# Toeplitz bands by predicated copies, four half batches fetched in SyncE's order, and passes on zeros ahead of the first convolution

## The chip, the core and the metric

The kernel runs on one core of a Trainium2 chip. The metric is the time of one execution on the device, in microseconds (us). The kernel before took 1273.2 us (median of 3 runs, 1272.89 to 1273.23). The engines are named as in the profile: PE is TensorE, DVE is VectorE, ACT is ScalarE, POOL is GpSimd and SP is SyncE, which only issues transfers.

## What is computed

Every token is a weighted sum of itself and the six tokens ahead of it, with softmax weights of its own for each of eight heads of 24 columns. The 28672 results then go through a mixture of eight experts: logits, a greedy assignment by falling logit with room for 3584 tokens in each expert, and two matrices per expert.

```python
def _attn_ref(x, weight):                      # x (8, 3584, 192), weight (8, 7)
    w = softmax(weight, axis=-1)               # per head
    x_pad = concatenate([zeros(B, 6, D), x], axis=1)
    x_unf = x_pad[:, idx, :].reshape(B, S, K, H, group)     # K = 7 taps, H = 8, group = 24
    return einsum('hk,bskhg->bshg', w, x_unf).reshape(B, S, D)

def _moe_ref(x, w_gate, w1, w2):               # x (28672, 192), w1 (8, 192, 1024), w2 (8, 1024, 192)
    logits = x @ w_gate
    for idx in argsort(-logits.flatten()):
        tok, e = idx // E, idx % E
        if assigned[tok] < 0 and counts[e] < cap:
            assigned[tok] = e
            counts[e] += 1
    for e in range(E):
        mask = assigned == e
        out[mask] = maximum(x[mask] @ w1[e], 0) @ w2[e]
```

## The kernel before

**Half batches.** The sequence work is cut into 16 half batches of 1792 tokens (NHB). In SBUF one is a tile X of 118 partitions by 16 windows by 192 columns: partitions 6 to 117 hold 112 successive tokens of each window, and partitions 0 to 5 hold the six tokens ahead of them (the halo). Four X tiles take turns. One half batch is fetched by three transfers: the halo (69 to 74 KB) and the first eight windows (688 KB) on SyncE's queue, and the other eight windows on ScalarE's (on SyncE's for half batch 0). Every row of 192 columns is a packet of 768 bytes.

**The Toeplitz matrices.** For each head, `toeplitz` builds a 118 by 128 matrix TH[h] that holds the head's seven weights on seven diagonals. The softmax of the weights (tile wb, with wm for maximum and sum) runs on VectorE and ScalarE. MK holds seven masks of one diagonal each. VectorE builds six heads' matrices, in pairs, by one multiplication and six multiply-adds each; ScalarE and GpSimd together build those of heads 1 and 5.

**The convolution.** `conv(i, mid)` runs over the eight heads. Per head TensorE multiplies TH[h] with X's 384 columns of that head into a PSUM bank cv, in two passes since the operands are fp32; `mid(h)` puts in other work; then ScalarE copies cv into the tile a (an evacuation). There are four cv banks and three tiles a. After the eighth head ScalarE issues the store of a to the DRAM tensor attn (1.38 MB, packets of 3 KB). VectorE transposes the a of one half batch while the next one is convolved, TensorE computes its logits (pl) a half batch later, and the logits are transposed (pt) into the table LT. Steps of the expert assignment (thresholds, counts) and, later, of the first expert tiles are put in by `hook`.

**Order.** The main loop calls `k.load(i + 3)` at the start of half batch i, so ScalarE issues its part of X of half batch i + 3 after the store of i - 1 and ahead of the first evacuation of i. Each engine works in the order in which its instructions are written. A transfer issued by SyncE or ScalarE signals one of eight semaphores, which are handed out in turn over both queues; the issue of a transfer waits until the one before it on the same semaphore has landed. An issuing engine does nothing else while it waits.

**The gate.** `gate_ops` loads the gate matrix wgr four times, into four groups of 32 partitions, and GpSimd copies each into its place in GF (in the trace c_mu).

After the loop come the experts' matrices (ph, px and y in the trace), which take most of the time; the change touches nothing of them.

## Time and profile before

| | |
|---|---|
| median of 3 runs | 1273.2 us |
| the profiled execution | 1268.0 us, of which the span is 1266.2 us |
| TensorE busy | 1222.0 us, 97% of the span |
| VectorE / ScalarE / GpSimd busy | 999.6 / 551.2 / 510.1 us |
| start of half batches 0, 1, 2, 3, 4 | 11.61, 20.34, 28.17, 37.79, 47.35 us |

The times of the trace count from the start of the span of that one execution. "Busy" of an engine counts its instructions' own durations, without the issuing of transfers and the waiting for semaphores. A wait is put down to what signalled last. Names such as L55 are lines; since one helper records every operation of the compute engines, most of them have line 55, and the tiles' names tell them apart. L188, L191 and L193 are the three transfers of X, L168 the gate's and L204 the store of a.

### The profile page before, as it was taken

The numbers are of one execution on the slowest core, as the hardware profiler recorded it, in microseconds if no ns is written. First come the engines' busy times: TensorE is split into PE (matmuls) and PEld (weight loads), VectorE is DVE, ScalarE is ACT, GpSimd is POOL, SyncE is SP. The second block draws the span as 40 slices with busy tenths as digits, with TensorE's granted clock in tenths as the row PEclk, the third lists the DMA queues.
The fourth block names the chain that finished last, engine by engine and source line by source line (L and its number), as shares of the span: only waits on it lengthen the run. The fifth ranks groups of instructions, "written<-read, shape, count | busy, mean of one in ns | idle before, by whom it ended". The sixth has DMA issues, their size and how long they took to land.

```text
span 1266.2 us, 21792 instructions
## 1 busy us (share of the span) xinstructions
PE 1222.0 (97%) x7839; PEld 1049.9 (83%) x7839; DVE 999.6 (79%) x2245; ACT 551.2 (44%) x1220; POOL 510.1 (40%) x504
## 2 busy tenths in 40 slices
PE   5889979999999999999999999999999999999997
PEld 2445558899889888887889999999999999999997
DVE  7398669999999989988857777777777777777772
ACT  4544645565544543643433333333333333333332
POOL 3000435364444443533244444444444444444422
PEclk9999989999999999999999999999999999999999
DMA  9999897999533343423653513242314132231100
GB/s 236 347 334 297 271 328 257 294 316 319 194 103 112 122 152 94 152 93 125 161 126 105 205 41 100 94 155 62 129 48 147 46 102 97 85 105 47 45 26 28
DMA packets 100579, 193.02 MB, mean 152 GB/s; under 512 B 19232, under 2 KB 64752, under 8 KB 96240
## 3 DMA queue, kind: packets, MB, share of 16 engines
q1 hardware_dynamic: 57856, 115.15, 28.1%
q0 software_dynamic: 21504, 44.07, 11.7%
q10 hardware_dynamic: 21104, 32.34, 7.8%
q8 instruction: 63, 1.03, 0.3%
q14 instruction: 52, 0.43, 0.1%
HBM read 116.02 MB, written 75.50 MB: 151 GB/s over the span
## 4 chain that ended last, share of the span: by engine, by line
PE 83%; DVE 7%; DMA 5%; issue 1%; POOL 1%; ACT 1%; SPq 1%; POOLq 0%; ACTq 0%; DVEq 0%
PE ph L55 38%; PE y L55 37%; PE cv L55 3%; PE bg L55 3%; DMA X<-in_x_dram 1%; PE px L55 1%; DVE X L55 1%; DMA raw<-in_moe_w_dram 1%; DVE hl L55 1%; DVE oa L55 1%; DVE aT L55 1%; DMA wgr<-in_moe_w_gate_dram 1%; PE pl L55 1%; DMA X<-otab 1%; POOL xg L1262 0%
## 5 line engine op out<-in xcount | busy, mean ns | idle before, releaser
L55 PE MATMUL y<-w,hh 128*128 128x384 f32 x1792 | 539.3, 356 | 0.0
L55 ACT ACTIVATE hh<-ph 128x512 fp32r<-128x512 f32 x448 | 268.1, 598 | 494.2 <-PE ph L55 493.9
L55 PE MATMUL y<-w,hl 128*128 128x192 f32 x1792 | 448.9, 251 | 0.0
L55 DVE SCALAR_TENSOR_TENSOR hl<-ph,hh 128x512 fp32r<-128x512 f32 x448 | 308.1, 688 | 140.6 <-ACT hh L55 136.6
L55 PE MATMUL ph<-xa,w 128*128 128x512 f32 x1344 | 395.7, 402 | 3.9 <-DVE hl L55 3.9
L55 PEld LDWEIGHTS y<-w,hl 128*128 128x128 f32 x1792 | 341.0, 190 | 15.1
L55 PEld LDWEIGHTS y<-w,hh 128*128 128x128 f32 x1792 | 336.4, 188 | 19.1 <-issue 2.3
L1337 POOL DMA_INDIRECT out_dram<-yo,ib x128 | 127.9, 999 | 288.4 <-DVE yo L55 278.6
L55 PEld LDWEIGHTS ph<-xa,w 128*128 128x128 f32 x1344 | 218.7, 189 | 24.6 <-DVE hl L55 5.2
L1337 POOL DMA_INDIRECT out_dram<-yo,ia x96 | 112.2, 1168 | 262.3 <-DVE yo L55 230.0
L55 DVE STREAM_TRANSPOSE xs<-xg 32x256 f32<-32x256 f32 x496 | 182.9, 369 | 8.5
L55 PE MATMUL ph<-xd,w 128*128 128x512 f32 x448 | 177.3, 396 | 1.5 <-DVE xd L55 1.5
L55 PE MATMUL ph<-xd,dl 128*128 128x512 f32 x448 | 174.5, 390 | 0.0
L1262 POOL DMA_INDIRECT xg<-attn,jb x128 | 137.8, 1076 | 40.9 <-issue 40.9
L1262 POOL DMA_INDIRECT xg<-attn,ja x96 | 110.2, 1147 | 32.1 <-issue 26.7
L55 ACT ACTIVATE yt<-y 128x192 f32<-128x192 f32 x224 | 73.6, 328 | 102.6 <-PE y L55 99.5
L55 PE MATMUL cv<-X,TH 118*128 118x384 f32 x256 | 99.6, 515 | 18.9 <-DVE TH L55 12.5
L55 DVE TENSOR_TENSOR yo<-y,yt 128x192 f32<-128x192 f32 x224 | 79.4, 354 | 40.8 <-ACT yt L55 38.1
L55 PEld LDWEIGHTS ph<-xd,w 128*128 128x128 f32 x448 | 84.2, 188 | 21.2 <-DVE xd L55 2.0
L55 PEld LDWEIGHTS ph<-xd,dl 128*128 128x128 f32 x448 | 84.3, 188 | 19.7
L55 PEld LDWEIGHTS cv<-X,TH 118*128 118x128 f32 x256 | 44.6, 194 | 51.8 <-issue 13.0
L55 ACT ACTIVATE a<-cv 128x384 f32<-128x384 f32 x128 | 59.7, 492 | 53.3 <-PE cv L55 32.0
(237 smaller groups left out, 900.4 us busy)
## 6 DMA issues: line engine op xcount, KB each, us to landing
w<-kw SPq DMA_DIRECT2D x16, 1536.0 KB
w<-kv SPq DMA_DIRECT2D x16, 1536.0 KB
attn<-a ACTq DMA_DIRECT2D x16, 1344.0 KB
kw<-w SPq DMA_DIRECT2D x48, 256.0 KB
kv<-w SPq DMA_DIRECT2D x32, 384.0 KB
X<-in_x_dram SPq DMA_DIRECT2D x17, 672.0 KB
X<-in_x_dram ACTq DMA_DIRECT2D x15, 672.0 KB
raw<-in_moe_w_dram SPq DMA_DIRECT2D x32, 192.0 KB
```

Of the source, the lines that this page charges most:

```text
L55: return f(*a, **k)
L1262: self.nc.gpsimd.indirect_dma_start(out=t[:, b], out_offset=None, in_=self.attn[0:rows], in_offset=bass.IndirectOffsetOnAxis(ap=idx[b], ax ...
L1337: st = self.nc.gpsimd.indirect_dma_start(out=self.out, out_offset=bass.IndirectOffsetOnAxis(ap=idx, axis=0), in_=o, in_offset=None, bounds ...
```

## The change

- VectorE sets a tile zb to zero, and TensorE runs 28 passes of 512 bf16 columns on it into the bank pt, ahead of everything else (`warm`).
- The seven diagonals are built only in a band: C has 38 columns per head and partition, and the seven weights are put into it by seven predicated copies, each for all eight heads (304 elements per partition), with MK as an integer mask. Four copies, two on VectorE and two on ScalarE, put C's four groups of 32 partitions in their places in TH, which GpSimd has zeroed whole. The multiply-adds on VectorE and the steps on ScalarE and GpSimd go.
- SyncE issues half batches 0 to 3 whole (halo and all 16 windows in two transfers), with one load of the gate matrix between 1 and 2. The four copies into GF read that one tile and run on VectorE.
- From i = 1 to 12, `load(i + 3)` still issues the halo and the first eight windows at the start of half batch i; ScalarE's part is issued in `mid(3)`, between the third and the fourth evacuation.

SyncE's first issues, before (X_180, X_188, X_278 and X_312 are half batches 0, 1, 2 and 3; a wait names a semaphore):

```order
L188 DMA X_180<-in_x_dram 6x15x192
L193 DMA X_180<-in_x_dram 112x8x192 x2
L191 DMA X_188<-in_x_dram 6x16x192
L193 DMA X_188<-in_x_dram 112x8x192
L168 DMA wgr_141<-in_moe_w_gate_dram 32x6x8 [waits DMAHW0_49]
L168 DMA wgr_141<-in_moe_w_gate_dram 32x6x8 [waits DMAHW1_49]
L168 DMA wgr_141<-in_moe_w_gate_dram 32x6x8 [waits DMAHW2_49]
L168 DMA wgr_141<-in_moe_w_gate_dram 32x6x8 [waits DMAHW3_49]
L188 DMA X_278<-in_x_dram 6x15x192 [waits DMAHW5_49]
L193 DMA X_278<-in_x_dram 112x8x192 [waits DMAHW6_49]
L191 DMA X_312<-in_x_dram 6x16x192 [waits DMAHW0_49]
L193 DMA X_312<-in_x_dram 112x8x192 [waits DMAHW2_49]
```

and with the change (half batches 0, 1, 2 and 3 are X_211, X_215, X_219 and X_223):

```order
L202 DMA X_211<-in_x_dram 6x15x192
L208 DMA X_211<-in_x_dram 112x16x192
L205 DMA X_215<-in_x_dram 6x16x192
L208 DMA X_215<-in_x_dram 112x16x192
L176 DMA wgr_143<-in_moe_w_gate_dram 32x6x8
L202 DMA X_219<-in_x_dram 6x15x192
L208 DMA X_219<-in_x_dram 112x16x192 [waits DMAHW0_49]
L205 DMA X_223<-in_x_dram 6x16x192 [waits DMAHW2_49]
L208 DMA X_223<-in_x_dram 112x16x192 [waits DMAHW4_49]
```

The gate's four loads, each with a wait, no longer stand ahead of half batch 2; semaphore 0 is there the one of the load of the weights (wb), 2 that of X of half batch 0 and 4 that of X of half batch 1.

ScalarE from the last evacuation of half batch 1 to the third of half batch 2, before (X_388 is half batch 5):

```order
L55 ACTIVATE a_357<-cv_384 128x16x24 [waits PE_49]
L204 DMA attn_62<-a_357 112x4x768 [waits DMAHW5_49,Activation_49]
L193 DMA X_388<-in_x_dram 112x8x192 [waits DMAHW7_49,DMAHW6_49]
L55 ACTIVATE a_392<-cv_393 128x16x24 [waits PE_49]
L55 ACTIVATE a_392<-cv_398 128x16x24 [waits PE_49]
L55 ACTIVATE a_392<-cv_410 128x16x24 [waits PE_49]
```

and with the change, to the fourth (X_352 is half batch 5):

```order
L55 ACTIVATE a_320<-cv_348 128x16x24 [waits PE_49]
L219 DMA attn_62<-a_320 112x4x768 [waits DMAHW3_49,Activation_49]
L55 ACTIVATE a_355<-cv_356 128x16x24 [waits PE_49]
L55 ACTIVATE a_355<-cv_361 128x16x24 [waits PE_49]
L55 ACTIVATE a_355<-cv_373 128x16x24 [waits PE_49]
L208 DMA X_352<-in_x_dram 112x8x192 [waits DMAHW6_49,DMAHW4_49]
L55 ACTIVATE a_355<-cv_377 128x16x24 [waits PE_49]
```

The load of half batch 5 stands behind three evacuations. It waited for the store of half batch 0 (semaphore 7) and for a part of X (6), and now waits for the halo of half batch 2 (6) and X of half batch 1 (4). The store of half batch 1 now waits for the halo of half batch 1. Behind these pieces the instructions of every engine stand in the same order as before, save for ScalarE's part of X in each half batch.

```diff
-    pmi = cst.tile([128, 128], I32, name="pmi")
-    P.iota(pmi, pattern=[[-1, 128]], base=0, channel_multiplier=1)
-    D0 = cst.tile([128, 128], BF, name="D0")
-    V.tensor_copy(D0, pmi)
+    zb = cst.tile([128, 512], BF, name="zb")
+    V.memset(zb, 0.0)
+    BW = 38
+    pmi = cst.tile([128, 7, BW], I32, name="pmi")
...
+    C = cst.tile([128, 8, BW], F32, name="C")
+    P.memset(C, 0.0)
     TH = cst.tile([128, 8, 128], F32, name="TH")
-    P.memset(TH[:, :, W:128], 0.0)
-    MK = cst.tile([128, 7, W], BF, name="MK")
-    for j in range(7):
-        V.tensor_scalar(MK[:, j], D0[:, 0:W], float(j), None, op0=OP.is_equal)
+    P.memset(TH, 0.0)
...
+    MK = cst.tile([128, 7, BW], I32, name="MK")
+    V.tensor_scalar(MK, pmi, pf, None, op0=OP.is_equal)
...
+    def warm(n):
+        ps = k.bank("pt")
+        for _ in range(n):
+            PE.matmul(ps, zb[:, 0:128], zb, start=True, stop=True)
...
         A.activation(wb, wb, AF.Exp)
-        load(1)
...
-        tk = cst.tile([128, 2, W], F32, name="tk")
-        for h in (1, 5):
-            A.activation(TH[:, h, 0:W], MK[:, 0], AF.Copy, scale=wb[:, h, 0:1])
-            for j in range(1, 7):
-                A.activation(tk[:, j % 2], MK[:, j], AF.Copy, scale=wb[:, h, j:j + 1])
-                P.tensor_tensor(TH[:, h, 0:W], TH[:, h, 0:W], tk[:, j % 2], op=OP.add)
-        for hs in ((0, 2), (3, 4), (6, 7)):
-            for j in range(7):
-                for h in hs:
-                    t = TH[:, h, 0:W]
-                    if j == 0:
-                        V.tensor_scalar(t, MK[:, 0], wb[:, h, 0:1], None, op0=OP.mult)
-                    else:
-                        V.scalar_tensor_tensor(t, MK[:, j], wb[:, h, j:j + 1], t, op0=OP.mult, op1=OP.add)
-    wgr = cst.tile([128, 6, 8], F32, name="wgr")
+        for j in range(7):
+            V.copy_predicated(C, MK[:, j, None, :].to_broadcast([128, 8, BW]), wb[:, :, j, None].to_broadcast([128, 8, BW]))
+        for a in (0, 3, 1, 2):
+            lo = 32 * a - 6
+            c0, c1 = max(lo, 0), min(32 * a + 32, W)
+            o, i = TH[32 * a:32 * a + 32, :, c0:c1], C[32 * a:32 * a + 32, :, c0 - lo:c1 - lo]
+            if a % 3:
+                V.tensor_copy(o, i)
+            else:
+                A.activation(o, i, AF.Copy)
...
-    wgr = cst.tile([128, 6, 8], F32, name="wgr")
+    wgr = cst.tile([32, 6, 8], F32, name="wgr")
...
+    def gate_load():
+        nc.sync.dma_start(wgr, wg.rearrange("(c f) e -> f c e", f=32))
     def gate_ops():
-        for pb in range(4):
-            nc.sync.dma_start(wgr[32 * pb:32 * pb + 32], wg.rearrange("(c f) e -> f c e", f=32))
         P.memset(GF, 0.0)
         for pb in range(4):
             q = slice(32 * pb, 32 * pb + 32)
-            P.tensor_copy(GF[q, :, 8 * pb:8 * pb + 8], wgr[q])
-        pi = cst.tile([128, 1], I32, name="pi")
-        P.iota(pi, pattern=[[0, 1]], base=0, channel_multiplier=1)
+            V.tensor_copy(GF[q, :, 8 * pb:8 * pb + 8], wgr)
...
-    def load(i):
+    def prep(i):
         t = X[i] = k.xp[i % 4].tile([118, 16, D], F32, name="X")
+        if i % 2 == 0:
+            P.memset(t[0:6, 0], 0.0)
+    def load(i, parts=(0, 1)):
+        t = X[i]
         b, hf = divmod(i, 2)
         o = x.offset + (b * 3584 + hf * 1792) * D
-        if hf == 0:
-            P.memset(t[0:6, 0], 0.0)
-            nc.sync.dma_start(t[0:6, 1:16], bass.AP(tensor=x.tensor, offset=o + (W - 6) * D,
-                                                    ap=[[D, 6], [W * D, 15], [1, D]]))
-        else:
-            nc.sync.dma_start(t[0:6], bass.AP(tensor=x.tensor, offset=o - 6 * D, ap=[[D, 6], [W * D, 16], [1, D]]))
-        for eng, w in ((nc.sync, 0), (A if i else nc.sync, 8)):
-            eng.dma_start(t[6:118, w:w + 8], bass.AP(tensor=x.tensor, offset=o + w * W * D, ap=[[D, W], [W * D, 8], [1, D]]))
+        if 1 not in parts or 0 in parts:
+            if hf == 0:
+                nc.sync.dma_start(t[0:6, 1:16], bass.AP(tensor=x.tensor, offset=o + (W - 6) * D,
+                                                        ap=[[D, 6], [W * D, 15], [1, D]]))
+            else:
+                nc.sync.dma_start(t[0:6], bass.AP(tensor=x.tensor, offset=o - 6 * D, ap=[[D, 6], [W * D, 16], [1, D]]))
+        for p in parts:
+            eng, w, n = {0: (nc.sync, 0, 8), 1: (A, 8, 8), None: (nc.sync, 0, 16)}[p]
+            eng.dma_start(t[6:118, w:w + n], bass.AP(tensor=x.tensor, offset=o + w * W * D, ap=[[D, W], [W * D, n], [1, D]]))
...
+        k.warm(28)
+        for i in range(4):
+            k.prep(i)
+            k.load(i, (None,))
+            if i == 1:
+                k.gate_load()
         k.toeplitz()
         k.gate_ops()
-        k.load(2)
         r.consts()
         for i in range(NHB):
-            if i + 3 < NHB:
-                k.load(i + 3)
+            if 1 <= i < NHB - 3:
+                k.prep(i + 3)
+                k.load(i + 3, (0,))
...
             def mid(h):
+                if h == 3 and 1 <= i < NHB - 3:
+                    k.load(i + 3, (1,))
```

## Rows read from the trace of the kernel before

**Rows 1.** The page's first part: busy us, share of the span, instructions.

```profile
PE 1222.0 (97%) x7839; PEld 1049.9 (83%) x7839; DVE 999.6 (79%) x2245; ACT 551.2 (44%) x1220; POOL 510.1 (40%) x504
```

**Rows 2.** Timeline of PE, convolution passes: start, us, what, [idle before it <-releaser].

```profile
11.61 6.45 PE L55 MATMUL cv<-X,TH 118*128 118x384 f32 x12 [11.61 <-DVE TH L55]
18.98 6.69 PE L55 MATMUL cv<-X,TH 118*128 118x384 f32 x20 [0.91 <-DVE TH L55]
28.17 1.53 PE L55 MATMUL cv<-X,TH 118*128 118x384 f32 x4 [2.50 <-DMA X<-in_x_dram]
...
34.22 1.56 PE L55 MATMUL cv<-X,TH 118*128 118x384 f32 x4 [1.89 <-ACT a L55]
...
43.78 1.56 PE L55 MATMUL cv<-X,TH 118*128 118x384 f32 x4 [1.90 <-ACT a L55]
...
47.35 1.45 PE L55 MATMUL cv<-X,TH 118*128 118x384 f32 x4
...
62.53 1.45 PE L55 MATMUL cv<-X,TH 118*128 118x384 f32 x4
```

**Rows 3.** Timeline of ACT; an ACTq row is the issue of a transfer.

```profile
4.96 0.39 ACTq L193 DMA_DIRECT2D X<-in_x_dram  x1
...
21.31 0.32 ACTq L204 DMA_DIRECT2D attn<-a  x1
...
33.68 2.02 ACT L55 ACTIVATE a<-cv 128x384 f32<-128x384 f32 x5 [7.49 <-DMA attn<-a]
...
43.24 2.02 ACT L55 ACTIVATE a<-cv 128x384 f32<-128x384 f32 x5 [4.59 <-DMA X<-in_x_dram]
```

**Rows 4.** Timeline of SP's issues: the last gate load and two loads of X.

```profile
10.83 0.31 SPq L168 DMA_DIRECT2D wgr<-in_moe_w_gate_dram  x1
...
17.40 0.31 SPq L193 DMA_DIRECT2D X<-in_x_dram  x1
...
20.59 4.42 SPq L188 DMA_DIRECT2D X<-in_x_dram  x1
```

**Rows 5.** Stretches: length, busy us of PE, PEld, DVE, ACT, POOL, clock, DMA share, GB/s.

```profile
6.00:9.00 3.00, 0.00 (x0) 0.00 (x0) 2.96 (x10) 2.17 (x7) 1.77 (x5) 1.00 1.11 258
18.90:25.70 6.80, 6.69 (x20) 3.69 (x20) 4.39 (x12) 4.01 (x9) 3.74 (x21) 1.00 1.11 230
26.00:48.00 22.00, 16.04 (x133) 8.45 (x134) 7.63 (x10) 7.95 (x23) 1.78 (x3) 1.00 1.07 361
48.00:66.00 18.00, 18.00 (x157) 9.23 (x155) 10.51 (x19) 9.13 (x25) 0.25 (x1) 1.00 1.05 330
66.00:110.00 44.00, 38.59 (x335) 20.24 (x334) 39.50 (x96) 21.63 (x57) 1.69 (x4) 1.00 1.04 332
```

**Rows 6.** Timeline of DVE: the last step of the softmax of the weights.

```profile
5.92 0.22 DVE L55 TENSOR_TENSOR wb<-wb,wm 128x56 f32<-128x56 f32 x1
```

**Rows 7.** Groups of DVE by shape, xcount | busy us, mean ns | idle before.

```profile
L55 DVE COPY_PREDICATED T<-r_oki,r_tl 128x8 f32<-128x8 int32 x5 | 0.9, 170 | 0.2
L55 DVE TENSOR_TENSOR asm<-asm,bg 128x256 f32<-128x256 f32 x1 | 0.4, 411 | 0.0
```

**Rows 8.** The chain from 186 to 200 us: five passes of 512 columns.

```profile
189.87 1.17 PE ph L55 x5
```

**Rows 9.** Tile cv, 11 to 18.2 and 18.9 to 26 us: ns min/median/max, first to last start.

```profile
L55 PE MATMUL cv<-X,TH x12: 486/847/977, 11.6 to 17.6; 118*128 118x384 f32 x12
L55 PE MATMUL cv<-X,TH x20: 486/486/561, 19.0 to 25.2; 118*128 118x384 f32 x20
```

**Rows 10.** DMA queues from 30 to 33 us: packets, MB, share (q10 ScalarE's, q1 SyncE's).

```profile
q10 hardware_dynamic: 598, 0.61, 60.0%
q1 hardware_dynamic: 589, 0.45, 47.3%
```

**Rows 11.** DMA queues from 5 to 10 us, the only one that moved packets.

```profile
q1 hardware_dynamic: 1746, 1.31, 111.0%
```

**Rows 12.** DMA queues from 23.2 to 26.4 us, the only one that moved packets.

```profile
q1 hardware_dynamic: 963, 0.73, 111.2%
```

More of the change, by code (lines that the diff above doesn't have):

```diff
@@ L124, in build @@
     nc.sync.dma_start(wb, bass.AP(tensor=weight.tensor, offset=weight.offset, ap=[[0, 128], [7, 8], [1, 7]]))
-    pmi = cst.tile([128, 128], I32, name="pmi")
-    P.iota(pmi, pattern=[[-1, 128]], base=0, channel_multiplier=1)
-    D0 = cst.tile([128, 128], BF, name="D0")
-    V.tensor_copy(D0, pmi)
-    TH = cst.tile([128, 8, 128], F32, name="TH")
-    P.memset(TH[:, :, W:128], 0.0)
-    MK = cst.tile([128, 7, W], BF, name="MK")
-    for j in range(7):
-        V.tensor_scalar(MK[:, j], D0[:, 0:W], float(j), None, op0=OP.is_equal)
+    zb = cst.tile([128, 512], BF, name="zb")
+    V.memset(zb, 0.0)
+    BW = 38
+    pmi = cst.tile([128, 7, BW], I32, name="pmi")
+    P.iota(pmi, pattern=[[-1, 7], [-1, BW]], base=6, channel_multiplier=1)
+    pi = cst.tile([128, 1], I32, name="pi")
+    P.iota(pi, pattern=[[0, 1]], base=0, channel_multiplier=1)
+    C = cst.tile([128, 8, BW], F32, name="C")
+    P.memset(C, 0.0)
+    TH = cst.tile([128, 8, 128], F32, name="TH")
+    P.memset(TH, 0.0)
+    pq = cst.tile([128, 1], I32, name="pq")
+    V.tensor_scalar(pq, pi, 96, None, op0=OP.bitwise_and)
+    pf = cst.tile([128, 1], F32, name="bandf")
+    V.tensor_copy(pf, pq)
+    MK = cst.tile([128, 7, BW], I32, name="MK")
+    V.tensor_scalar(MK, pmi, pf, None, op0=OP.is_equal)
     wm = cst.tile([128, 8], F32, name="wm")
+    def warm(n):
+        ps = k.bank("pt")
+        for _ in range(n):
+            PE.matmul(ps, zb[:, 0:128], zb, start=True, stop=True)
     def toeplitz():
@@ L238, in build @@
     k.load, k.conv, k.transp, k.logits, k.logits_t = load, conv, transp, logits, logits_t
-    k.toeplitz, k.gate_ops = toeplitz, gate_ops
+    k.toeplitz, k.gate_ops, k.gate_load, k.prep, k.warm = toeplitz, gate_ops, gate_load, prep, warm
     return k
@@ L1547, in hook @@
                     todo.pop(0)()
-        k.load(0)
+        k.warm(28)
[4 more added lines that the diff above has]
+                k.gate_load()
         k.toeplitz()
         k.gate_ops()
-        k.load(2)
         r.consts()
         for i in range(NHB):
-            if i + 3 < NHB:
-                k.load(i + 3)
+            if 1 <= i < NHB - 3:
+                k.prep(i + 3)
+                k.load(i + 3, (0,))
             if i == 4:
```

## The prediction, made before the changed kernel had run

> **What bounds the kernel now.** I read the busy shares first: TensorE works 1222.0 of 1266.2 us [rows 1], so only time in which it waits, or runs at a lower clock, can be won without taking work from it. The change touches the first 60 us, so next come TensorE's convolution passes in order of time [rows 2]. A row there is a run of passes, and the bracket names the wait ahead of it. Half batch 0 starts at 11.61 and waits for the Toeplitz matrices (TH); half 2 starts at 28.17 after 2.50 us for X; inside halves 2 and 3 TensorE waits 1.89 and 1.90 us for ScalarE's evacuation (a); half 4 starts at 47.35, half 6 at 62.53. Two undisturbed half batches so take 15.18 us, while halves 2 and 3 took 47.35 - 28.17 = 19.18. Four microseconds are lost there.
>
> ScalarE's rows tell why [rows 3]. It evacuates and also issues transfers, in one order. Ahead of half 2's evacuations it stood 7.49 us, and ahead of half 3's 4.59, because the load of X three halves on, issued there, waited for the semaphore of an earlier transfer. With four PSUM banks TensorE runs ahead at first and loses only the rest. SyncE has the same trouble: a halo load of X stood 4.42 us from 20.59 [rows 4], and SyncE's part of half 2's X, issued only at 17.40, is late for half 2. From 48 to 66 us TensorE is busy 18.00 of 18.00 us, and from 66 to 110 VectorE 39.50 of 44 [rows 5]: behind half 4 the change alters no order but one ScalarE issue per half batch, so I take it that whatever half 4 gains goes through to the end.
>
> **The change, part by part.**
>
> *First start.* X of half 0 has landed at about 10.8: the last gate load, whose issue waits for it, goes out at 10.83 [rows 4]. TH now follows the last step of the softmax, which starts at 5.92 and takes 0.22 [rows 6], so 6.14. Seven predicated copies of 304 elements are new. The nearest rows: a predicated copy of 8 elements takes 170 ns, a plain two-operand pass of 256 takes 411 [rows 7], that is 0.97 ns per element, so 0.17 + 296 x 0.00097 = 0.46 us each; were an element to cost double, 0.74. Seven take 3.2 to 5.2, and two copies each on VectorE and ScalarE (up to 0.46 each, side by side) 0.9: TH stands at 10.3, at most 12.3. I take the lower price, since the plain pass also reads two operands. Of the 42 VectorE steps and the ScalarE and GpSimd ones that go, only those for the first matrices stood ahead of 11.61; the rest ran beside half 0.
>
> *Running on zeros.* 28 passes of 512 columns from about 1.4 us. A pass of that width takes 1.17 / 5 = 0.234 us in the midst of the program [rows 8]; at half the clock, 0.47. So they end between 8.0 and 14.6; I take the middle and let X decide: half 0 starts at 10.8. In the kernel before, the first passes took up to 977 ns, median 847, against 486 in half 1 [rows 9]: TensorE had been idle until then, and 977 to 486 is as its two levels, 1.2 and 2.4 GHz. If the zeros cure that, half 0 takes what half 1's passes took: 20 in 6.69, so 16 in 5.35 [rows 2], and ends at 16.2. If they cure nothing it takes 20.34 - 11.61 = 8.7 and ends at 19.5.
>
> *X in order.* One ring, reads alone, moved 258 and 230 GB/s [rows 5]; I take 0.25 MB/us. A half batch is 1.45 MB, so 5.8 us: X of half 1 lands at 16.6, half 1 runs 16.6 to 22.0 (at most 24.9 without the warm start), and X of half 2 lands at 22.4 if nothing joins it. Half 2 so waits for X by at least 0.4 us, and everything above is covered by that wait: **the Toeplitz build and the zeros are worth nothing here but the cover**, and a start of half 0 at 14.6 would still let half 2 begin at 25.3. The three gate loads taken away and the one kept (32 rows of 32 bytes) come after X of half 1; their four copies, now on VectorE (c_mu), stand ahead of nothing before the first transposes.
>
> What joins it is the store of half 0, issued at about 16.6 instead of 21.31 [rows 3]. It has 448 packets of 3 KB. Where both queues have work, they moved packet for packet, 598 to 589 [rows 10]. Then 448 packets of X (0.34 MB) go with 1.38 MB of store: 1.72 MB at 361 GB/s [rows 5] is 4.8 us where the X alone needs 1.4, so half 2 starts at 22.4 + 3.4 = 25.8. If the store starts late (below) it is 24.1 or 22.4. I take 25.8, because the row with both kinds of transfer is the nearer one. **Half 2 is 2.4 us earlier than 28.17.**
>
> *Halves 2 and 3.* X of half 3 is issued when that of half 1 has landed, 16.6, ahead of all of ScalarE's later transfers. From 25.8 it needs 1.45 MB / 0.25 = 5.8 at the most, 31.6, and half 2 computes until 25.8 + 7.6 = 33.4. It is hidden with 1.8 us to spare, as long as what ScalarE issues later (the second half of X of half 4, the store of half 1) doesn't push in. Twice in this trace such a transfer stood behind a backlog of SyncE's: none of ScalarE's packets moved from 5 to 10 us, with a load of X issued at 4.96, nor from 23.2 to 26.4, with the store issued at 21.31 [rows 3, 11, 12]. That is my ground for it. ScalarE's loads then wait for transfers that are long done, so 7.49 and 4.59 go. What is new is that the store of half 1 and the load of half 5 wait for the semaphores of X of halves 1 and 2. By the arrivals above these are in, so 0; at the most 1.9, what a held issue cost TensorE before [rows 2]. I take 0.8, below the middle, because the arrivals are old. Halves 2 and 3 take 15.2 + 0.8 = 16.0 instead of 19.2: **3.2 us**.
>
> *Later loads.* In 12 half batches ScalarE issues its half of X after the third evacuation instead of before the first. One issue takes 0.39 us either way when it is not held, as that at 4.96 [rows 3]. Cover: the held time less TensorE's loss was 7.49 - 1.89 = 5.6 and 4.59 - 1.90 = 2.7 us; below 2.7 a hold costs nothing. I price it at nothing. Supply: half 6 needs seven half batches and four stores, 10.2 + 5.5 = 15.7 MB, by 57.0. What can move is 4.2 to 16.6 us and then 40.4 us at 330 GB/s [rows 5], 13.3, so 17.5 MB.
>
> Sum: 2.4 + 3.2 = 5.6 us. The profiled execution took 1268.0 (span 1266.2) and so becomes 1262.4; against the median of the runs, 1273.2, the forecast is **1267.6 us**. The profiled one lies 5.2 below the median; I carry the difference over.
>
> **The rivals.**
>
> *The queues share evenly from each issue (R1).* Then X of half 3 alternates with everything that ScalarE has issued. X of halves 2 and 3 (2.9 MB) go with two stores and two half loads (4.1 MB), 7.0 MB from 16.6 on: 36.1 at 361 GB/s, 37.9 at 330. Half 3 starts at 37.0 instead of 33.4, half 4 at 45.4, 1.95 us earlier than before: **1271.2**. For it speaks the even count of [rows 10], against it the two late starts. The Trainium skill, "DMA: Bandwidth & Descriptors", section "Queues, rings and completion order", says that each DMA engine takes turns between the queues that have work for it, packet by packet. By that rule alone R1 is the forecast, 1271.2 instead of 1267.6; the trace agrees with it from 30 to 33 us and not in those two stretches. Chance 0.22.
>
> *Reads first (R2).* ScalarE's store waits until X of half 2 is in. Half 2 at 22.4, half 3 at 30.0, half 4 at 38.4: 9.0 us, **1264.2**. For it: the late starts. Against: more backlog is issued ahead than then. Chance 0.12.
>
> *Slower (R3).* ScalarE's load inside the half batch stands for a transfer not yet in, with five evacuations queued behind it, and TensorE fills its four banks. A hold of 3.5 us costs 3.5 - 2.7 = 0.8; twelve cost 9.6, less 5.6: **1277.2**. It decides from 0.47 us each. For it: both late waits of [rows 2] were of this kind. Against: the transfers it waits for are then a half batch old. Chance 0.09.
>
> *It doesn't do what it says (R4).* X of half 2 lands as before; only the holds go: 28.17 + 16.0 = 44.2, 3.2 us, **1270.0**. Chance 0.05.
>
> **How the numbers follow.** The forecast's own case keeps 0.52; with half 2 at 24.1 to 26.3 (half a microsecond for ScalarE's load of half 4, should it join at the end) and the hold at 0 to 1.9 it reaches from 1265.1 to 1269.2. Range: R2 below and most of R1 above, 1263.2 to 1272.5; what is left out is R3 and the outer ends of R1 and R2. A measurement here tells 0.2% from no change, so faster ends at 1270.65. Faster: 0.52 + 0.12 + 0.05 = 0.69; within: R1, 0.22; slower: R3, 0.09.
>
> **What would show it.** The starts of halves 0, 2, 3 and 4 in the changed profile: 10.8, 25.8, 33.4, 41.8. Half 3 at 36 or later, waiting for X, is R1; half 2 at 22.4 is R2; waits for a inside every half batch are R3. Predicated copies near 0.46 us and half 0 in 5.4 us confirm the first two terms, though they carry none of the sum. It would be wrong if half 4 came early and the end did not, that is, if something behind half 4 waits for a time of its own.

## The result, and the profile after

The changed kernel is slightly slower: 1276.35 us (median of 22 runs, 1274.48 to 1281.27) against 1273.07 for the kernel before (22 runs beside them), a ratio of 1.0021 with a 95% interval of 1.0011 to 1.003. The forecast was 1267.6. Twice more, on other chips, the ratio came out at 1.0017 (1.0006 to 1.0029) and 1.003 (1.0017 to 1.0043).

TensorE's convolution passes in order of time, in the changed kernel (start, us, what, idle time before):

```profile
1.20 8.11 PE L55 MATMUL pt<-zb 128*128 128x512 bf16 x28 [1.20 <-DVE zb L55]
10.56 5.40 PE L55 MATMUL cv<-X,TH 118*128 118x384 f32 x16 [1.25 <-ACT TH L55]
17.85 7.09 PE L55 MATMUL cv<-X,TH 118*128 118x384 f32 x16 [1.89 <-DMA X<-in_x_dram]
26.28 1.53 PE L55 MATMUL cv<-X,TH 118*128 118x384 f32 x4 [1.34 <-DMA X<-in_x_dram]
...
39.53 2.90 PE L55 MATMUL cv<-X,TH 118*128 118x384 f32 x4 [5.43 <-DMA X<-in_x_dram]
43.38 2.85 PE L55 MATMUL cv<-X,TH 118*128 118x384 f32 x4
...
50.30 1.45 PE L55 MATMUL cv<-X,TH 118*128 118x384 f32 x4
```

Set against [rows 2], half 0 is 1.0 us earlier and half 2 is 1.9 earlier; the waits of 1.89 and 1.90 us for a have gone. But half 3 waits 5.43 us for X and starts 1.7 us later than before (37.79), and half 4 starts 2.95 later (47.35). Half 3 alone took 50.30 - 39.53 = 10.8 us instead of 7.6: its first runs of four passes take 2.9 us instead of 1.5. Half 1 was slow too, 7.09 us for 16 passes where half 0 took 5.40, but the wait for X of half 2 covered that. The stretches say why (length; busy us of PE, PEld, DVE, ACT, POOL; granted clock; DMA share; GB/s):

```profile
17.80:26.20 8.40, 7.09 (x16) 3.69 (x16) 5.53 (x16) 3.93 (x8) 0.94 (x6) 0.80 1.07 331
34.00:39.50 5.50, 0.10 (x1) 0.00 (x0) 3.94 (x5) 0.66 (x2) 1.79 (x3) 0.97 1.08 327
39.50:46.70 7.20, 7.17 (x40) 3.32 (x40) 0.00 (x0) 1.91 (x4) 0.00 (x0) 0.55 1.01 329
50.30:69.00 18.70, 18.70 (x160) 9.66 (x162) 10.70 (x19) 10.63 (x27) 0.25 (x1) 1.00 1.00 309
```

TensorE stood from 34.1 to 39.5, and then ran at a granted clock of 0.55, near the lower of its two levels (1.2 of 2.4 GHz), for 7 us. The DMA was busy all the time and moved 327 GB/s: it carried other things than what half 3 needed. From half 4 to half 12 the distance to the kernel before stays at 2.95 us (in half 7, 72.31 becomes 75.27). That is about what the medians of the runs differ by, but it is this trace's figure alone: in the other two traces of the changed kernel half 4 starts at 46.63 and 48.31 us, against 47.35 and 47.49 in the two traces of the kernel before, and on both of those chips the changed kernel is slower all the same. The two profiled executions themselves lie 10.4 us apart (1278.45 and 1268.0), so most of their difference comes later.

What the DMA carried ahead of half 3 is seen in its queues from 18 to 24 us (packets, MB, share; q1 is SyncE's queue, with X of halves 2 and 3; q10 is ScalarE's):

```profile
q1 hardware_dynamic: 1171, 0.89, 64.0%
q10 hardware_dynamic: 329, 1.01, 43.9%
```

and from 24 to 32 us:

```profile
q10 hardware_dynamic: 1195, 1.51, 57.4%
q1 hardware_dynamic: 1498, 1.14, 50.7%
```

The store of half 0 already moves a megabyte ahead of 24 us, and behind it ScalarE's queue goes on beside SyncE's, 1195 packets to 1498, where the prediction had it stand back. ScalarE's timeline answers to [rows 3]:

```profile
16.51 0.35 ACTq L219 DMA_DIRECT2D attn<-a  x1
...
29.32 0.32 ACTq L208 DMA_DIRECT2D X<-in_x_dram  x1
...
41.19 0.49 ACT L55 ACTIVATE a<-cv 128x384 f32<-128x384 f32 x1 [6.39 <-PE cv L55]
```

The store is issued at 16.51 in place of 21.31, the load of half 5 goes out at once, and ScalarE's one long wait is now for TensorE, no longer 7.49 and 4.59 us for transfers. And X of half 3 does not land in one piece. The trace has sixteen signals for such a transfer, and the profile counts sixteen DMA engines, so I read them as one signal per engine. These are the times of the sixteen signals of X of half 3 in three kernels (the second and third are experiments, below):

```
changed kernel             31.4 31.7 32.0 32.0 32.4 32.5 32.9 33.2 33.6 34.0   37.0 37.8 38.0 38.2 38.6 39.4
changed loads alone        27.1 27.3 27.3 27.3 27.5 27.6 28.1 28.1 28.8 29.1   32.9 33.8 34.0 34.4 35.1 35.4
halos row by row, no hold  29.2 29.4 29.5 29.5 29.5 30.1 30.2 30.4 30.5 30.5   30.9 30.9 31.0 31.1 31.8 32.2
```

In the first two lines ten engines are done and the other six follow three to six microseconds later. A halo has six rows, and of its own seven signals six are late (half 3's halo in the changed kernel: one at 18.0, six from 25.3 to 27.9). The other two traces of the changed kernel have the same late end without the gap: there the sixteen signals come from 33.5 to 38.8 and from 31.8 to 38.9 us.

### The profile page after: what moved, and what is told of

Read it like the earlier page. It is cut to its first block, busy times and chain, and to the rows that moved or that the text cites. A ratio compares the mean times of both kernels' runs of the same rounds, so it can differ in the third digit from the quotient of the medians.

```text
span 1276.7 us, 21768 instructions
## 1 busy us (share of the span) xinstructions
PE 1231.3 (96%) x7867; PEld 1052.5 (82%) x7867; DVE 992.5 (78%) x2212; ACT 548.0 (43%) x1208; POOL 509.1 (40%) x489
## 3 DMA queue, kind: packets, MB, share of 16 engines
q1 hardware_dynamic: 59904, 117.19, 28.5%
q0 software_dynamic: 21504, 44.07, 11.6%
## 4 chain that ended last, share of the span: by engine, by line
PE 87%; DVE 6%; DMA 4%; issue 1%; ACT 1%; SPq 1%; another core or an unknown queue 0%; POOL 0%; POOLq 0%; DVEq 0%; ACTq 0%
PE ph L55 39%; PE y L55 38%; PE cv L55 5%; DMA X<-in_x_dram 3%; PE bg L55 3%; PE px L55 1%; PE pl L55 1%; DVE X L55 1%; DVE aT L55 1%; DVE oa L55 1%; DVE hl L55 1%; DMA raw<-in_moe_w_dram 1%; DVE sl L55 0%; ACT w L55 0%
## 5 line engine op out<-in xcount | busy, mean ns | idle before, releaser
L1277 POOL DMA_INDIRECT xg<-attn,jb x128 | 138.0, 1078 | 40.9 <-issue 40.9
L1277 POOL DMA_INDIRECT xg<-attn,ja x96 | 113.0, 1177 | 29.1 <-issue 26.1
```

Source lines behind the costliest of these rows:

```text
L1277: self.nc.gpsimd.indirect_dma_start(out=t[:, b], out_offset=None, in_=self.attn[0:rows], in_offset=bass.IndirectOffsetOnAxis(ap=idx[b], ax ...
```

## The experiments

Every ratio is to the kernel before, timed beside it on the same chip; the four or two kernels of a group shared a chip. The chips' own times for the kernel before were 1270.1, 1268.4, 1273.3, 1267.6 and 1275.9 us.

### First chip: the parts of the change

**The loads alone** (old Toeplitz build, no zeros):

```diff
-        k.warm(28)
-            V.copy_predicated(C, ...)
+            ... the build of the kernel before
```

> The loads as changed, the Toeplitz build as before, no zeros. Theory A: the loss sits in X of half batch 3. It shares the DMA packet for packet with stores and loads issued later on ScalarE's queue, lands near 39.5 us as in the changed kernel, TensorE stands some 5 us and then runs at the lower clock for some 7 us. By A half 3 starts at 38.5 to 40.5 after a wait for X of over 3 us, half 4 at 49.5 to 51, and the time is 2.5 to 3.5 us over the kernel before, as the changed kernel's. Theory B: the build by predicated copies or the zeros cost the time (a lower clock later on). By B half 4 starts where it did before or earlier, at 42 to 47.5, and the time is 0 to 5 us below the kernel before.

Measured: half 3 at 35.51 after 1.97 us for X, half 4 at 44.80, 1266.64 us, ratio 0.9967 (0.9953 to 0.9981). A is wrong in its number: the wait is there, but shorter, and on this chip this part by itself is a gain. B's direction is right, though not yet its reason.

**The build and the zeros alone** (loads as before):

```diff
+        k.warm(28)
         k.load(0)
         k.toeplitz()
```

> The new Toeplitz build and the zeros, all loads as before. Theory A: half 0 starts near 10.8, half 2 still waits for X until about 28, halves 3 and 4 start near 37.5 and 47 with the two waits for ScalarE's evacuations of 1.9 us, and the time is that of the kernel before within 1 us. Theory B: the time is 2 us or more above the kernel before.

Measured: 1269.76 us, ratio 1.0004 (0.9991 to 1.0017). Half 2 starts at 30.93 (28.17 before), half 4 at 47.77. A quicker start of half 0 and 1 thus delays half 2. The store of half 0 comes earlier here too, and ScalarE's next load holds its evacuations:

```profile
24.35 4.36 PE L55 MATMUL cv<-X,TH 118*128 118x384 f32 x8 [3.62 <-ACT a L55]
30.93 2.90 PE L55 MATMUL cv<-X,TH 118*128 118x384 f32 x4 [2.23 <-DMA X<-in_x_dram]
```

**Without the zeros:**

```diff
-        k.warm(28)
```

> The changed kernel without the 28 passes on zeros. Theory A: half 0 takes 8 to 9 us instead of 5.4, its store is issued some 3 us later, half 2 still starts at 24.5 to 26.5, since X decides, half 3 at 37 to 40, half 4 at 47.5 to 50.5; the time is that of the changed kernel, at most 2.5 us less. Theory B (the zeros cost clock): half 3 runs at the full clock in spite of its wait, and the time is 3 us or more below the changed kernel's.

Measured: half 2 at 24.31, half 3 at 37.19 after 5.05 us, half 4 at 47.01, 1267.45 us, ratio 0.9977 (0.9963 to 0.9991). From 18 to 24 us no packet of the store moves; the store's first packet goes at 24.4 us and not at 20.5. Neither theory as written: half 3 still ran at the lower clock after its wait (0.59 from 34 to 39.5), against B, yet the time fell further than A allowed (5.6 us by the ratios, the changed kernel having been timed on another chip). This gave theory C: the quick half 0 harms through its early store. The store is not the whole of it: X of half 3 was in at 37.0 us instead of 39.4, and since half 2 was early too, the wait was nearly as long.

**Zeros ahead of half 3 as well:**

```diff
+            if i == 3:
+                k.warm(24)
             k.conv(i, mid)
```

> The changed kernel with 24 more passes on zeros ahead of half batch 3, in the time in which TensorE waits for X (24 x 0.22 = 5.2 us). It tells the wait from the clock. Theory A: half 3 starts at 39.5 as in the changed kernel but takes 7.6 instead of 10.8 us, half 4 starts at 47.1 instead of 50.3, and the time falls by 3 us, to that of the kernel before. If the low clock of that stretch does not come from the wait, half 3 takes 10.8 us again and the time stays the changed kernel's or rises.

Measured: half 3 at 37.99, half 4 at 46.27, 1264.42 us, ratio 0.9958 (0.9944 to 0.9972).

```profile
32.52 5.34 PE L55 MATMUL pt<-zb 128*128 128x512 bf16 x24 [0.37 <-ACT LT L55]
37.99 1.53 PE L55 MATMUL cv<-X,TH 118*128 118x384 f32 x4
```

Behind a TensorE that was kept running, the same passes take 1.53 us and not 2.90: half 3 takes 8.3 instead of 10.8. With TensorE kept running the low clock did not come, here and in two more traces with such zeros (below). A bare wait brought it in most traces and not in all: behind 3.15 us on the second chip half 3 ran at 1.00. The time fell by more than the 3 us that this explains; see the third chip.

### Second chip: is it the early store?

**The changed kernel again**, unedited:

> The changed kernel as it is, beside the other runs on one chip. Theory C, formed from the runs without the zeros: a quicker half 0 issues its store earlier, 16.5 us instead of 20 or later, so that the store's 3 KB packets pass one for one with the X of halves 2 and 3; half 3 then waits some 5 us and runs at the lower clock. By C the store is again under way before 24 us, half 3 starts at 37.5 to 40 and half 4 at 48 to 50.5, and the time is 1 to 4 us over the kernel before. If the changed kernel's first result was an accident of its chip, it comes out below the kernel before, as the one without the zeros did.

Measured: store from 20.3 us, half 3 at 38.97 after 3.15 us, half 4 at 46.63, 1270.48 us, ratio 1.0017 (1.0006 to 1.0029). The loss is no accident of one chip; half 4 came earlier than I had expected, since the clock fell ahead of half 3 here (0.79 from 26 to 34 us) and not in it.

```profile
38.97 1.53 PE L55 MATMUL cv<-X,TH 118*128 118x384 f32 x4 [3.15 <-DMA X<-in_x_dram]
...
46.63 1.45 PE L55 MATMUL cv<-X,TH 118*128 118x384 f32 x4
```

In this trace half 4 starts 0.7 us earlier than in that of [rows 2], and yet the runs are 0.17% slower. So the start of half 4 does not explain the loss on this chip.

**X of halves 2 and 3 on both queues, ahead of the stores:**

```diff
-            k.load(i, (None,))
+            k.load(i, (None,) if i < 2 else (0,))
...
         k.toeplitz()
+        for i in (2, 3):
+            k.load(i, (1,))
```

> The changed kernel, but of half batches 2 and 3 the second eight windows are issued by ScalarE behind its copies to TH, ahead of every store on its queue. Theory C: no store packet moves before X of halves 0 to 3 is nearly in, at 26 to 29 us; half 2 starts at 22.5 to 25, half 3 at 30 to 33.5 without a wait over 1 us and at the full clock, half 4 at 38 to 43, and the time is 4 to 9 us below the kernel before. If the supply of the DMA as a whole is the bound, half 4 waits instead and starts at 44 or later, and the time is at most 3 us below the kernel before.

Measured: half 2 at 25.94, half 3 at 33.97 with no wait for X, half 4 at 41.63, 1265.7 us, ratio 0.9981 (0.9969 to 0.9993). Half 4 is where the forecast had put it (41.8).

```profile
25.94 1.53 PE L55 MATMUL cv<-X,TH 118*128 118x384 f32 x4 [1.52 <-DMA X<-in_x_dram]
...
33.97 1.53 PE L55 MATMUL cv<-X,TH 118*128 118x384 f32 x4 [0.21 <-PE pt L55]
```

With half of X ahead of the stores half 3 waits 0.21 us for the operation before it and for no transfer, and its passes run at once in 1.53 us. It was close: the other half of its X, which SyncE could issue only at 21.4 us, was in at 33.7, and the store's first packet moved at 22.0 and not at 26 to 29 as expected. The time won is less: 2.4 us of 5.7.

**The stores of halves 0 and 1 later:**

```diff
-        A.dma_start(attn[...], a[0:W])
+        held.append((i, a))
+        while held and (i > 1 or held[0][0] < i):
+            j, s = held.pop(0)
+            A.dma_start(attn[j ...], s[0:W])
```

> The changed kernel with the store of half 0 issued behind the last evacuation of half 1, and that of half 1 behind the last of half 2. Theory C: X of halves 2 and 3 has the DMA to itself until some 25 us, half 2 starts at 22 to 24.5, half 3 at 30 to 33.5, at the full clock and with little wait; half 3's first evacuation needs no old store, half 4's first waits for that of half 1, so half 4 starts at 39 to 44. The time is 3 to 8 us below the kernel before. If X of half 3 is late for another reason than the stores, half 3 starts at 36 or later.

Measured: half 3 at 33.60 without a wait, half 4 at 42.27, but half 5 at 53.2 and half 6 at 64.0 (62.5 before); 1267.73 us, ratio 0.9993 (0.9977 to 1.0009). C holds for half 3: its X was in at 33.5 instead of 39.4 us. X of half 2 was no earlier, 25.8 us, although no packet of ScalarE's queue had moved before 26.7. What the DMA did not do early it does later: half 4 waits for evacuations, half 5 for X.

```profile
51.54 0.91 PE L55 MATMUL cv<-X,TH 118*128 118x384 f32 x2 [2.04 <-ACT a L55]
53.23 2.90 PE L55 MATMUL cv<-X,TH 118*128 118x384 f32 x4 [0.66 <-DMA X<-in_x_dram]
```

**Zeros only ahead of half 3** (the edits of the third and fourth together):

> The changed kernel without the 28 first passes on zeros, and with 24 ahead of half 3. Theory C: half 3 starts near 37 as without any zeros, but runs at the full clock, so half 4 starts near 45 instead of 47, and the time is 4 to 6 us below the kernel before. If the clock of half 3 carried nothing to the end, the time is that without any zeros, 3 us below the kernel before.

Measured: the last signal of X of half 3 at 36.3, but the zeros ran until 38.6; half 3 at 38.46, 7.6 us long, half 4 at 46.05; 1267.39 us, ratio 0.9987 (0.9975 to 0.9999). Half 3 was held up by its own zeros, which ate what the clock gave.

### Third chip: the six late engines

**Halos row by row:** the halos of halves 1 to 3 go as six transfers of one row, on GpSimd's queue.

```diff
+        if 1 <= i < 4 and (None in parts or 0 in parts):
+            z = 1 - hf
+            for q in range(6):
+                P.dma_start(t[q:q + 1, z:16], bass.AP(..., ap=[[D, 1], [W * D, 16 - z], [1, D]]))
+        elif ...
```

> The changed kernel with the halos of half batches 1 to 3 fetched row by row: six transfers of one partition each, on GpSimd's queue, so that they are spread over the DMA engines. Theory D, formed from the arrivals in the changed kernel's trace: a transfer's sixteen signals come one per DMA engine; ten of X of half 3 came from 31.4 to 34.0 us and six from 37.0 to 39.4, a halo has only six rows, and its late signals are six in number, so six engines carry all halos and X waits for them. By D the sixteen signals of X of half 3 come within 3 us of one another, the last at 34 to 36.5 us; half 3 starts then instead of at 39 to 39.5, half 4 at 42 to 45, and the time is 2 to 6 us below the kernel before. If the six late signals have another cause, they stay late by 4 us or more, half 3 starts at 38 or later, and the time is again over that of the kernel before.

Measured: the sixteen signals of X of half 3 come from 31.1 to 34.4 us, those of half 2 from 21.8 to 23.1 (21.2 to 26.0 in the changed kernel). That is as D has it. But half 3 starts at 37.06, the time is 1274.17 us, ratio 1.0 (0.9989 to 1.0012). The three halos no longer take semaphores in turn with SyncE's and ScalarE's other transfers, so ScalarE's load of half 5 now takes the one of X of half 3, and waits for it in front of half 2's last five evacuations:

```profile
34.87 0.87 ACT L55 ACTIVATE a<-cv 128x384 f32<-128x384 f32 x2 [8.19 <-DMA X<-in_x_dram]
```

```profile
35.41 1.65 PE L55 MATMUL cv<-X,TH 118*128 118x384 f32 x2 [5.14 <-ACT a L55]
```

The first fence is ScalarE's timeline, the second TensorE's: one wait was taken away and another, as long, put in.

**Both queues and halos row by row** (the edits of two kernels above):

> The kernel with X of halves 2 and 3 on both queues ahead of the stores, with the halos of halves 1 to 3 row by row besides: a candidate for the best. By theory D half 1 starts near 18, half 2 at 23.5 to 25.5 instead of 25.9, half 3 without a wait for X, half 4 at 39 to 41.5, and the time is 3 to 7 us below the kernel before. If the halos don't matter, half 2 starts at 25.9 again and the time is 1 to 3.7 us below.

Measured: half 1 at 18.0, half 2 at 23.1, half 3 at 31.4, half 4 at 39.0, for these two the earliest of all; 1271.19 us, ratio 0.998 (0.9967 to 0.9992). The starts are as D has them; the gain is 2.5 us and not the 3 to 7 expected.

**The loads alone and halos row by row:**

> The loads as changed with the old Toeplitz build and no zeros, and with the halos of halves 1 to 3 row by row. Without the rows X of half 3 had ten signals by 28.7 us and the last six from 33.1 to 35.4, and half 3 started at 35.5. By theory D the last signal comes by 31 us, half 3 starts at 33 to 34 without a wait, half 4 at 41 to 42.5, and the time is 3 to 7 us below the kernel before. If the halos don't matter, half 3 starts at 35 to 36 with its wait.

Measured: half 1 only at 28.0, ratio 1.0008 (0.9995 to 1.0021). Its starts and its time say nothing on D: the old build adds up two heads' matrices on GpSimd, and these steps stood behind the issues of eighteen transfers (TensorE waited 7.18 us for them). Its signals do. No store packet moved before 31.6 us here, and none before 26.4 in the loads alone (fourth chip, below). The sixteen signals of X of half 3 came from 26.3 to 28.6 us, where the loads alone had ten by 29.1 and six more by 35.4: the ten hardly moved, the six came with them. What this does not part is the spreading from the change of queue, since the rows went to GpSimd's queue and no run sent a halo there whole.

**Zeros ahead of half 3, again:**

> The kernel with 24 more passes on zeros ahead of half 3 once more, on the chip of these three. Its first time was 5.3 us below the kernel before, where the clock alone explains 3 us below the changed kernel. If that was chance, the time comes out between 2 us below and 1 us above the kernel before; if the zeros there do more than keep the clock, 4 us or more below.

Measured: half 3 at 41.4, half 4 at 49.0, 1275.59 us, ratio 1.0014 (0.9998 to 1.0029). Its first result, 5.3 us below, did not come again. Of the 7 us between the two results 2.7 are in the start of half 4 (46.27 in the first trace): half 2 began late and at a clock of 0.78, and the zeros ran until 41.6 although X was in at 39.0. The rest is not explained.

### Fourth chip: chip or kernel, and the hold

**The kernel before**, for a trace of its own:

> The kernel before, for a trace on the same chip. Half 2 starts at 27 to 29, half 3 at 36 to 39, half 4 at 46 to 49; the ratio is 1 within 0.1%.

Measured: halves 2, 3, 4 at 28.5, 38.0, 47.5; ratio 1.0005 (0.9995 to 1.0014). Its trace agrees with that of [rows 2] within 0.5 us through the convolutions.

**The changed kernel, third time:**

> The changed kernel once more. By theories C and D half 3 starts at 38 to 40 after a wait for X, half 4 at 46 to 50.5 and the time is 1 to 4 us above the kernel before. If the loss belonged to single chips, it comes out at or below the kernel before.

Measured: half 3 at 39.07 after 3.65 us, half 4 at 48.31, 1270.8 us, ratio 1.003 (1.0017 to 1.0043).

**The loads alone, again:**

> The changed loads with the old build and no zeros, beside the changed kernel on one chip. By theory C the later first half leaves the DMA to X for longer: the store of half 0 starts after 24 us, half 3 starts at 35 to 37, half 4 at 44 to 46, and the time is 2 to 5 us below the changed kernel's. If the first result was the chip's, it is within 1 us of the changed kernel's.

Measured:

```profile
25.61 1.53 PE L55 MATMUL cv<-X,TH 118*128 118x384 f32 x4 [0.23 <-issue]
...
35.56 2.10 PE L55 MATMUL cv<-X,TH 118*128 118x384 f32 x4 [2.13 <-DMA X<-in_x_dram]
...
44.81 1.45 PE L55 MATMUL cv<-X,TH 118*128 118x384 f32 x4
```

Half 3 at 35.56 after 2.13 us for X, half 4 at 44.81, 1267.81 us, ratio 0.9993 (0.9981 to 1.0005). That is 3.0 us less by the medians (1270.8 - 1267.81) than the changed kernel beside it, as C has it, but no longer clearly below the kernel before. The queues from 18 to 24 us:

```profile
q1 hardware_dynamic: 1795, 1.36, 111.5%
```

Only X moves there, 1.36 MB instead of 0.89. The parts that were meant to help, the quick build and the zeros, cost 3 us together when put on the new loads.

**Halos row by row, X of half 5 wholly on SyncE:**

```diff
-                k.load(i + 3, (0,))
+                k.load(i + 3, (None,) if i == 2 else (0,))
...
-                if h == 3 and 1 <= i < NHB - 3:
+                if h == 3 and 1 <= i < NHB - 3 and i != 2:
```

> The changed kernel with the halos of halves 1 to 3 row by row and X of half 5 wholly on SyncE, so that no evacuation of half 2 stands behind a load. By theory D the last signal of X of half 3 comes by 33 to 35.5 us, half 3 starts then without a wait for a, half 4 at 41 to 44, and the time is 2 to 5 us below the changed kernel's. If half 3 still starts at 37 or later with X in, something else holds it.

Measured: signals of X of half 3 from 29.2 to 32.2 (the third line above), half 3 at 32.29 after 1.48 us, 7 us before the changed kernel's. D holds. But half 4 only at 44.6, and a ratio of 1.0006 (0.9994 to 1.0018): the next load of ScalarE, that of half 6, now stands before half 3's evacuations. TensorE's timeline, then ScalarE's:

```profile
32.29 1.53 PE L55 MATMUL cv<-X,TH 118*128 118x384 f32 x4 [1.48 <-DMA X<-in_x_dram]
...
42.93 1.65 PE L55 MATMUL cv<-X,TH 118*128 118x384 f32 x2 [3.58 <-ACT a L55]
```

```profile
42.39 0.87 ACT L55 ACTIVATE a<-cv 128x384 f32<-128x384 f32 x2 [6.63 <-DMA X<-in_x_dram]
```

### Fifth chip: do the zeros harm by themselves?

**X on both queues, again:**

> X of halves 2 and 3 on both queues ahead of the stores, with the zeros, once more. By theory C half 3 starts at 33 to 35 without a wait over 1 us, half 4 at 41 to 43, and the time is 1 to 4 us below the kernel before, as on the other chip.

Measured: halves 2, 3, 4 at 26.05, 34.01 and 41.68, within 0.11 us of the second chip's; yet 1277.79 us, ratio 1.0016 (1.0003 to 1.003), where it had been 0.9981.

**The same without the first zeros:**

> The same without the 28 first passes on zeros. By theory C the zeros harm only through the store of half 0; here no store comes ahead of X, so half 2 starts at 25 to 27 and half 3 at 33 to 35 as with the zeros, and the time is within 1.5 us of it. If the zeros harm by themselves, it is 2 us or more below the version with them.

Measured: halves 2, 3, 4 at 25.3, 33.1, 40.9; 1276.37 us, ratio 1.0006 (0.9991 to 1.002), 1.4 us below the version with them. Within what C expects, where no store comes ahead of X; C's other expectation, a gain, failed for both.

So the start of half 4 is not the time. For the version on both queues, the 5.8 us won by half 4 against the trace on the fourth chip shrink to 4.3 by half 7, to 2.9 by half 13 and to 1.3 at the last head of half 15. Part of this is again a wait for a (1.01 us in half 5), part the clock, in a stretch that has nothing to do with the change. From 118 to 130 us the rows of the kernel before (fourth chip), the loads alone (again) and the version on both queues (again) are:

```profile
118.00:130.00 12.00, 11.65 (x133) 8.02 (x133) 9.95 (x21) 5.50 (x14) 0.00 (x0) 1.00 0.90 278
```

```profile
118.00:130.00 12.00, 11.65 (x113) 7.01 (x112) 9.13 (x19) 3.52 (x10) 0.00 (x0) 0.72 0.99 312
```

```profile
118.00:130.00 12.00, 11.65 (x109) 7.71 (x108) 8.46 (x18) 5.00 (x12) 0.00 (x0) 0.86 0.98 312
```

TensorE is equally busy in all three, after the same pause of 0.35 us, and does less at the lower clock. What is lost behind half 15 on some chips I did not find out. No version here is shown to beat both kernels: the one on both queues with halos row by row has the lowest ratio that stands (0.998), from one chip, and the same kernel on two chips differed by up to 0.56%.

## Why the prediction was wrong

*First start: right.* Half 0 at 10.56 (10.8 forecast). The predicated copies take 501 ns (0.46 us forecast from [rows 7]); TH, not X, came last by a little. VectorE's group (count, busy us, mean ns, idle before):

```profile
L55 DVE COPY_PREDICATED C<-MK,wb 128x304 f32<-128x304 int32 x7 | 3.5, 501 | 0.3
```

*Zeros: right in their size, wrong in their worth.* 28 passes in 8.11 us, over at 9.3 (8.0 to 14.6 forecast), and half 0 in 5.40 (5.35 forecast). I called them worth nothing here but the cover. They cost: with the zeros half 0's store is issued at 16.5, and without them its first packet goes 4 us later, while X has the DMA alone. The loads alone against the changed kernel, 3.0 us on one chip, is the price of the quick build and the zeros together.

*X of half 2: right in its number, by luck.* 26.28, 26.4 and 26.0 in three traces, 25.8 forecast. The sum was 22.4 for X alone and 3.4 for the store beside it. But where no packet of ScalarE's queue moved before 26.4 us, X of half 2 was in at 25.5 (loads alone, fourth chip) and 25.8 (stores later), and with the halos row by row and no store packet until 23.8 it was in at 22.6. So the 22.4 was right for spread halos, and in the place of the store's 3.4 us stood the six late signals, for which the prediction had no term. (One of the two rows for "one ring, reads alone" is misread: from 18.9 to 25.7 us 731 packets of ScalarE's queue moved as well. The other, 258 GB/s from 6 to 9 us, is one ring's.)

*X of half 3: the step that failed.* "It is hidden with 1.8 us to spare" put X in at 31.6; its last signal came at 39.4. The ground given, that ScalarE's transfers stand behind SyncE's backlog, held for about 4 us (issued at 16.51, first packet at 20.5) and not longer. That was R1, which had 0.22: from 24 to 32 us 1195 packets of ScalarE's queue went beside 1498 of SyncE's. The Trainium skill, "DMA: Bandwidth & Descriptors", section "Queues, rings and completion order", says that each DMA engine takes turns between the queues that have work for it, packet by packet; by that rule alone R1 would have been the forecast, and these two counts, 1195 and 1498, agree with it in the main. But R1 put half 3 at 37.0, with all DMA engines alike; it started at 39.5. Ten signals were in by 34.0, and six came by 39.4. With the halos spread the six came with the others, the last at 34.4 beside an early store and at 28.6 without one; with the stores later and the halos whole it came at 33.5. Both terms were thus missing, the sharing and the six late engines. The profile's sums over all engines hide that a transfer ends with its slowest one.

*Halves 2 and 3: 16.0 us forecast, 24.0 measured* (26.28 to 50.30; 20.2 and 22.3 in the other two traces). The held loads went, as forecast: no wait for a is left there. In their place came 5.4 us for X, and 3.2 for the clock behind that wait, which no rival had priced. Zeros in the wait took the low clock away (8.3 and 7.6 us instead of 10.8).

*Later loads: right* in the changed kernel, where half 4 to half 12 keep their distance. In two kernels with the halos row by row, where the semaphores fell otherwise, the same kind of issue held evacuations for 8.2 and 6.6 us: R3's mechanism, once in each and not twelve times.

*"Whatever half 4 gains goes through to the end": the second step that failed.* It seems to fit the loss in the first trace (2.95 us, 2.7 by the runs), but that is luck: on the second chip half 4 was 0.7 us early and the time 2 us over. It fails for gains too: half 4 was 5.8 us earlier with X on both queues, and the time 2.4 us less on one chip and 2.0 more on another. The late X of half 3 thus accounts for the gain that did not come by half 4 (50.3, 46.6 and 48.3 us in three traces, 41.8 forecast); why the time is over that of the kernel before on all three chips stays open. That the supply which I had counted as enough (17.5 MB for 15.7) left too little room for the order in which it comes is argued, not shown.

*The clock over the whole run* is the nearest that the record has to a cause. The mean granted clock of the timed runs was 0.9907 to 0.9913 for the changed kernel on three chips, 0.9932 to 0.9946 for the same loads without the zeros (with the new build or the old), and 0.9933 to 0.9942 for the kernel before. A difference of 0.0025 of 1270 us is 3.2 us, an estimate that takes TensorE as the limit throughout. In the traces the granted clock over the first 50 us is 0.90, 0.97 and 0.93 for the changed kernel and 1.00 in both traces of the kernel before. The slow first passes of [rows 9] are no part of these figures: the clock column shows 1.00 from 11.6 to 18.1 us, so that the prediction's reading of them as the lower level rests on their duration alone. That the zeros lower the clock is not shown either. Without them the first 50 us had 0.93 too, and the version on both queues, with the zeros, had 0.9931 over its runs on one chip (kernel before 0.9934) and 0.9913 on another (kernel before 0.9942, the same without the zeros 0.9928).

## What to carry to other kernels

Where transfers bound a stage, starting its first compute earlier also starts its stores earlier, and they can take the transfer engines from the loads that the next step needs; look at what each queue moves in the stretch ahead of the wait before speeding up a start. Look at the first and the last signal of a transfer, not its mean: a small transfer that is spread over few engines can make a large one behind it late. A term that comes out right is no proof of its reason: look in a run where the reason is absent. An issue on a computing engine is a wait in waiting: each change in the number of transfers hands the semaphores out anew, and the hold turns up elsewhere.

## What the runs showed that I had not expected

- X of half 3 was signalled by ten engines within 2.6 us and by the other six up to 5.4 us after those; with the halos row by row all sixteen came within 2.3 to 3.3 us, in three traces.
- After a wait of 5.43 us TensorE's passes ran at a granted clock of 0.55 for 7 us; after 3.15 us (second chip) half 3 ran at 1.00, and from 118 to 130 us the clock fell to 0.72 in one trace and stayed at 1.00 in another behind the same pause. So the price of a wait is not its length alone.
- The same kernel's ratio to the kernel before moved from 0.9958 to 1.0014 and from 0.9981 to 1.0016 between chips, beyond the intervals of each. Only the verdict on the changed kernel was the same on three chips.
